# Head sums of the second half by accumulating DMAs instead of matmuls, with six weight loads held in pairs

## The chip, the cores and the metric

The kernel runs on one core of a Trainium2 chip. The metric is the device time of one execution in microseconds (us). Each kernel was also run once under the hardware profiler; numbers "from the profile" or "from the trace" belong to that one execution, and its span (first to last instruction) is about 2 us shorter than the time. Five engines work at once: TensorE (PE, matmuls), VectorE (DVE, elementwise), ScalarE (ACT, evictions and activations), GpSimd (POOL, here mostly an issuer of DMAs) and SyncE (SP, an issuer of DMAs).

## The reference

```python
x = A_x                                        # (1, 2048, 512), bf16
g = sigmoid((x * gate_w).sum(-1))              # one gate per position
# A: attention of 32 heads of 16; position s looks at s, s-2, ..., s-14 (8 offsets)
q, k, v = split(x @ wqkv)
logits  = einsum("bhsd,bhswd->bhsw", q, k[gathered]) * scale      # masked before 0
o       = einsum("bhsw,bhswd->bhsd", softmax(logits), v[gathered])
a       = o @ wo
# B: an MLP over the sequence axis
h = layernorm(x)                               # (2048, 512)
u = gelu(h^T @ w1 + b1)                        # w1: 2048 x 1792
b = (u @ w2 + b2)^T                            # w2: 1792 x 2048
return g * a + (1 - g) * b
```

The attention needs no large matmul besides the projections: each logit is a sum of 16 products. DVE does these products; PE does projections, both MLP matmuls and the output projection.

## The kernel before

The program records every operation with what it reads and writes. A list scheduler, which knows only estimated durations, then fixes the order on each engine, and semaphores are put in. So an engine works strictly through its list: an operation that must wait holds up all that stand behind it, on a DMA-issuing engine too.

The attention is worked in two halves of 1024 positions. For each half DVE forms products of q and shifted k in buffers `PB` of 128 x 8192 bf16, and adds the four slices of a head (`qk`, `qadd`). What is left is a sum over four neighbouring partitions, one per head. Before, PE does it for both halves, with a 0/1 matrix `RP` of 32 columns, and ACT copies the result out of PSUM:

```python
def f_sum(h, b0, with_gate):
    def fn(e):
        if with_gate:
            ...                                # 16 matmuls of the gate, first half only
        for wp in range(4):
            for c in range(4):                 # sum over 4 partitions: 128 rows -> 32 heads
                ins = e.matmul(ps[32*c:32*c+32, 4 + wp, :], lhsT=RP,
                               rhs=sub(PB[b0], ...), start=True, stop=True, tile_position=(0, 32*c))
        return ins
    return fn
...
A("pe",  f_sum(h, b0, h == 0), ...)
A("act", act(LOG[h], ps[:, 4:8, :], AF.Copy), 1.9, reads=LGB, writes=["log%d" % h], ...)
# then on DVE and ACT: max, subtract, exp, sum, normalise -> ATT[h]
for c in range(4):                             # "weight copies": one head's row to its 4 partitions
    prev = sch.dma("pool", ... e.dma_start(AVW[h] part c, ATT[h] rows 32c..32c+31, 4 times) ...)
```

Then come eight attention units of 256 positions. A unit is one product of 128 x 8192 (`m`), an addition of its halves (`a`, 128 x 4096), and two more (`b`, `c`). The result feeds the output projection of two output tiles: unit 4 feeds tiles 8 and 9. For three units the addition `a` is an accumulating DMA of 1 MB instead of a DVE instruction:

```python
AVD = (3, 4, 5)
def av_mult(u):
    AV(tt(pv, shifted V, AVW[...], ALU.mult), 4.4, ...)
    if u in AVD:
        sch.dma("pool", ... e.dma_start(pw(0, 4), pw(4, 4), accum_op=ALU.add) ...)
def av_add4(u):
    if u not in AVD:
        AV(tt(pw(0, 4), pw(0, 4), pw(4, 4), ALU.add), 2.25, ...)
```

W2 comes in eight loads of 0.92 MB on the queue of SP. Each waits only for its buffer to be free. The output tiles are stored from the same queue, through four store buffers: ACT cannot evict a tile before the store that used its buffer four tiles earlier has landed.

```python
def ld_w2(j):
    w1ld[7 + j] = load("w2_%d" % j, W2S[j], w2v[:, :, 256*j:256*j+256], ..., after=[w1ld[6 + j]])
def finish_tile(i):
    PE(f_wo(i, bank, 0, D), ..., ["ot%d" % (i // 2), "wo"], ...)         # output projection
    A("act", act(OUTS[:, i % 4, :], ps[:, bank, :], AF.Identity, ...))   # eviction
    sch.dma("sp", ... e.dma_start(outv[:, i, :], OUTS[:, i % 4, :]) ...) # store
```

Of the kernel before, what the change touches and what calls it, by code (L numbers as in the profile page):

```python
# [12 lines left out]
S = 2048  # L13
# [56 lines left out]
class _Sched:  # L70
# [73 lines left out]
    def _pass(self, ops, extra, dma_bw, dma_lat):  # L144
# [21 lines left out]
        dma_free = 0.0  # L166
# [8 lines left out]
        while nleft:  # L175
            best = None
            for e in self.ENGS:
                lst = ready[e]
                if not lst:
                    continue  # L180
                bo = None
                bk = None
                for op in lst:
                    st = max(clock[e], rtime[op.idx])
                    if op.table is not None and loaded is not None and op.table != loaded:
                        st += 1.3
                    k = (st, -bl[op.idx] + 3.0 * op.prio, op.idx)
                    if bk is None or k < bk:
                        bk = k
                        bo = op  # L190
                if best is None or bk < best[0]:
                    best = (bk, bo)
            assert best is not None, "scheduler deadlock (cyclic deps?)"
            st = best[0][0]
# [6 lines left out]
            if op.is_dma:  # L201
                clock[e] = st + op.dur
                xs = max(st + 0.3, dma_free)
                xd = max(op.nbytes / dma_bw, 0.05)
                dma_free = xs + xd
                op.end = max(dma_free, clock[e]) + dma_lat
            else:
                op.end = st + op.dur
                clock[e] = op.end
# [98 lines left out]
def bass_gated_mix__sliding_local_dilated__mixer_token_mlp__prompt_kernel(nc, A_x, A_wqkv, A_wo, B_x, B_w1, B_b1, B_w2, B_b2, gate_w, out, dbg=None):  # L308
    with contextlib.ExitStack() as es:
# [11 lines left out]
        for b in range(3):  # L321
# [42 lines left out]
        W1H = [view(n_, BF16, [(256, NST), (1, 256)], extra=k_ * W1N)  # L364
               for n_, k_ in (("W1", 0), ("W1", 1), ("W1", 2), ("XT", 0), ("XT", 1), ("W1", 0), ("W1", 1))]
        W1R = ["w1s0", "w1s1", "w1s2", "w1x0", "w1x1", "w1s0", "w1s1"]

        def w2view(name, extra=0):
            return view(name, BF16, [(256, NFT), (1, 256)], extra=extra)
# [166 lines left out]
        def ld_w1(j):  # L536
            w1ld[j] = load("w1_%d" % j, W1H[j], w1v[:, :, 256 * j:256 * j + 256], S * 256 * 2, [W1R[j]] + (XTALL if j in (3, 4) else []), order=j < 3,
                           after=[w1ld[j - 1]] if j > 3 else [])

        def ld_w2(j):  # L540
            w1ld[7 + j] = load("w2_%d" % j, W2S[j], w2v[:, :, 256 * j:256 * j + 256], F * 256 * 2, ["w2_%d" % j] + W2ALIAS[j], order=False,
# [40 lines left out]
        def f_q0(hb, dt):  # L582
            c0, c1 = ((0, 256), (256, 512), (0, 512))[hb]

            def fn(e):
                ins = None
                for dl in range(4):
# [26 lines left out]
        pe_q0(2, 3)  # L614
# [46 lines left out]
        kb0 = [bank_() for dl in range(2)]  # L661
        for k_ in range(2):
            for dl in range(2):
                PE(f_proj(1, dl, 0, kb0[dl], 2 * k_, 2 * k_ + 2), 0.44, XT0 + ["wk%d" % k_], ["b%d" % kb0[dl]], "pjk%d_0_%d" % (dl, k_))
                if k_ == 1:
                    evac(1, dl, 0, kb0[dl])
        for dl in range(2, 4):
            proj(1, dl, 0)
# [7 lines left out]
        for dl in range(4):  # L676
# [3 lines left out]
            if dl == 1:  # L680
                PE(f_tb, 0.06, ["b1r", "b2r", "gwr", "ident"], ["b3"], "t_b12")
                A("dve", lambda e: e.tensor_copy(out=GWREP, in_=sub(psb(3), 544, [(1, 4), (0, 32)])), 0.2, reads=["b3"], writes=["gwrep"], name="gwrep", prio=-20)
                A("dve", lambda e: e.tensor_copy(out=B1C, in_=psb(3)[:, 512:512 + NFT]), 0.15, reads=["b3"], writes=["b1c"], name="b1c", prio=-20)
                A("dve", lambda e: e.tensor_copy(out=B2C, in_=psb(3)[:, 528:528 + NST]), 0.15, reads=["b3"], writes=["b2c"], name="b2c", prio=-20)
# [20 lines left out]
        for t in range(NST):  # L705
            A("dve", (lambda t_: lambda e: e.tensor_scalar(out=X[:, t_, :], in0=X[:, t_, :], scalar1=col(RSTD, t_), scalar2=col(NMR, t_),  # L706
                                                           op0=ALU.mult, op1=ALU.add))(t), 0.33,
              reads=["rstd", "nmr", "st%d" % t], writes=["x%d" % t], name="ln%d" % t, prio=-10)


        def f_sum(h, b0, with_gate):
            def fn(e):
                ins = None
                if with_gate:
                    for dt in range(4):
                        for c in range(4):
                            ins = e.matmul(ps[32 * c:32 * c + 32, 3, :], lhsT=GWREP[:, dt, :],  # L717
                                           rhs=sub(XT, dt * S + c * UT_, [(HS, 2), (1, UT_)]),
                                           start=(dt == 0), stop=(dt == 3), tile_position=(0, 32 * c))
                for wp in range(4):  # L720
                    for c in range(4):
                        ins = e.matmul(ps[32 * c:32 * c + 32, 4 + wp, :], lhsT=RP, rhs=sub(PB[b0], (c // 2) * 4096 + 2 * wp * 512 + (c % 2) * UT_, [(512, 2), (1, UT_)]),  # L722
# [4 lines left out]
        LGB = ["b4", "b5", "b6", "b7"]  # L727
        PLAN = {0: (0, 1, 2), 1: (1, 2, 0)}
        PS = [["p%d_%d" % (b_, s_) for s_ in range(2)] for b_ in range(3)]
        qkd = {}  # L730
        for h in range(2):
            bb = PLAN[h]

            def qk(dl, b_, s_, h=h):
                sb = 2 * h + s_
                A("dve", tt(sub(PB[b_], s_ * 4096, [(512, NW), (1, 512)]), sub(QH[h], dl * HS + s_ * 512, [(0, NW), (1, 512)]),
                            sub(KH[h], dl * KR + PAD + s_ * 512, [(-2, NW), (1, 512)]), ALU.mult), 2.25,
                  reads=["q%d_%d" % (dl, sb), "k%d_%d" % (dl, sb)] + (["k%d_%d" % (dl, sb - 1)] if s_ else ["khalo" if h else "kpad"]),
                  writes=[PS[b_][s_]], name="qk%d_%d_%d" % (h, dl, s_))

            def qadd(x_, y_, s_, h=h):
                A("dve", tt(sub(PB[x_], s_ * 4096, [(1, 4096)]), sub(PB[x_], s_ * 4096, [(1, 4096)]), sub(PB[y_], s_ * 4096, [(1, 4096)]), ALU.add), 2.25,
                  reads=[PS[y_][s_]], writes=[PS[x_][s_]], name="qa%d_%d%d_%d" % (h, x_, y_, s_))
# [12 lines left out]
            for s_ in range(2):  # L756
                qk(3, bb[1], s_)
                qadd(bb[2], bb[1], s_)
            for s_ in range(2):
                qadd(bb[0], bb[2], s_)  # L760
            b0 = bb[0]
            A("pe", f_sum(h, b0, h == 0), 1.2 + (1.0 if h == 0 else 0), reads=PS[b0] + ["rp"] + ((XTALL + ["gwrep"]) if h == 0 else []),
              writes=LGB + (["b3"] if h == 0 else []), name="sum%d" % h, prio=-100, delay=0.2)
            if h == 0:
                A("act", act(E32, ps[:, 3, :], AF.Relu, scale=-1.0, bias=ZMAX), 0.6, reads=["b3"], writes=["e32"], name="zclip")
                A("act", act(EB, E32, AF.Exp, scale=-1.0, bias=ZMAX), 0.6, reads=["e32"], writes=["eb"], name="zexp", table=LOGEXP)
            A("act", act(LOG[h], ps[:, 4:8, :], AF.Copy), 1.9, reads=LGB, writes=["log%d" % h], name="lev%d" % h, prio=-30)
            if h == 0:
                A("dve", tt(psub(LOG[0], 0, 32, 0, [(UT_, NW), (1, PAD)]), psub(LOG[0], 0, 32, 0, [(UT_, NW), (1, PAD)]), MASK, ALU.add), 0.2,
                  reads=["mask"], writes=["log0"], name="msk", prio=-30)  # L770
            TR = ["s4", "s2", "s1"]
            A("dve", tt(M4, LOG[h][:, 0:4, :], LOG[h][:, 4:8, :], ALU.max), 0.65, reads=["log%d" % h], writes=["s4"], name="mx4_%d" % h, prio=-30)
            A("dve", tt(M2, M4[:, 0:2, :], M4[:, 2:4, :], ALU.max), 0.4, reads=["s4"], writes=["s2"], name="mx2_%d" % h, prio=-30)
            A("dve", tt(M1, M2[:, 0, :], M2[:, 1, :], ALU.max), 0.25, reads=["s2"], writes=["s1"], name="mx1_%d" % h, prio=-30)
            A("dve", tt(LOG[h], LOG[h], sub(M1, 0, [(0, NW), (1, UT_)]), ALU.subtract), 1.2, reads=["s1"], writes=["log%d" % h], name="msub%d" % h, prio=-30)
# [7 lines left out]
            A("dve", tt(ATT[h], ATT[h], sub(RB, 0, [(0, NW), (1, UT_)]), ALU.mult), 1.2, reads=["rb"], writes=["att%d" % h], name="nrm%d" % h, prio=-30)  # L783
# [3 lines left out]
            for c in range(4):  # L787
# [3 lines left out]
                               reads=["att%d" % h], writes=["avw%d_%d" % (h, c)] + al, after=[prev] if prev else [], name="av%d_%d" % (h, c))  # L791
                al = []
# [16 lines left out]
        AVD = (3, 4, 5)  # L809
        AVB = (2, 0, 1)  # L810
        avlast = [None]

        def AV(fn, dur, **kw):
            avlast[0] = A("dve", fn, dur, after=[avlast[0]] if avlast[0] else [], **kw)

        def av_parts(u):
            b_ = AVB[u % 3]
# [17 lines left out]
        def av_add(u):  # L835
            res, pv, pw = av_parts(u)
            AV(tt(pw(0, 2), pw(0, 2), pw(2, 2), ALU.add), 1.19, writes=res, name="avb%d" % u)
            AV(tt(OT[:, u], pv[:, 0], pv[:, 1], ALU.add), 0.66, reads=res, writes=["ot%d" % u, OTRES[u]], name="avc%d" % u)

        todo = []  # L840
        for u in range(8):
            av_mult(u)
            if todo and todo[0] + 2 <= u:
                av_add(todo.pop(0))
            if u in AVD:
                todo.append(u)
            else:
                av_add4(u)
                if todo and u == 7:
                    av_add(todo.pop(0))  # L850
                av_add(u)


        def f_ph2(ft, bank, half):
            def fn(e):
                ins = None
                for st in range(8 * half, 8 * half + 8):
                    ins = e.matmul(ps[:, bank, :], lhsT=W1H[ft // 2][:, st, 128 * (ft % 2):128 * (ft % 2) + 128], rhs=X[:, st, :],  # L858
                                   start=(st == 0), stop=(st == NST - 1))
# [3 lines left out]
        MLPB = [1, 2, 0, 1, 2, 0, 3, 1, 2, 0, 3, 1, 2, 0]  # L863
        for ft in range(NFT):
            bank = MLPB[ft]
            for half in range(2):
                PE(f_ph2(ft, bank, half), 1.735, ["x%d" % t for t in range(8 * half, 8 * half + 8)] + [W1R[ft // 2]], ["b%d" % bank],
                   "ph2_%d_%d" % (ft, half))
            A("act", act(UT[:, ft, :], ps[:, bank, :], AF.Gelu_apprx_tanh, bias=col(B1C, ft)), 0.7,
              reads=["b%d" % bank, "b1c"], writes=["ut%d" % ft] + (["wq0", "wq1", "wq2", "wq3", "wk0", "wk1", "wv"] if ft == 0 else []), name="gel%d" % ft, table=GELU)  # L870
            if ft % 2 == 1 and ft // 2 + 5 <= 6:
# [147 lines left out]
```

## Time and profile before

| before | value |
|---|---|
| time | 165.56 us, median of 3 (165.08 to 166.12) |
| span in the profile | 163.0 us |
| PE busy | 158.6 us, 97% |
| DVE busy | 151.1 us, 93% |
| last attention addition on DVE ends | 157.4 us |
| last matmul starts | 160.2 us |

This is the page of the kernel before. The second line gives each engine's busy time. The rows show 40 slices of the span: busy tenths of PE and DVE (9 is 90% or more) and the granted PE clock in tenths of full speed. The last line is the chain of work that ended last, by engine.

```profile
span 163.0 us, 1989 instructions
...
PE 158.6 (97%) x793; PEld 77.2 (47%) x808; DVE 151.1 (93%) x126; ACT 70.2 (43%) x100; POOL 12.0 (7%) x36
...
PE   7999999999999999999999999999999999999993
DVE  1789999999999999999999999999999999999961
...
PEclk9999999999999999999999999999999999999999
...
PE 97%; ACT 1%; issue 1%
...
```

PE and DVE are both full, but the chain that decides the end is 97% PE. The end of that chain of waits (start, duration, what ran):

```profile
...
152.13 3.06 PE ps L885 x28
155.19 4.33 PE ps L894 x20
159.54 1.34 ACT arena L453 x2
...
```

Lines L885 (second MLP matmul) and L894 (output projection) follow each other with no wait up to 159.5 us; only an eviction and a store come after. DVE, by contrast, is one unbroken group in its timeline from 83 to 157.4 us (start, duration, group; an idle would start a new line):

```profile
...
83.09 74.32 DVE L450 TENSOR_TENSOR arena<-arena 128x4096 bf16<-128x4096 bf16 x41
...
```

And the view of waits (who, for whom: us in total, times, longest) has next to nothing for PE and DVE between the start and the last tile; ACT waits much, but for PE, which costs nothing:

```profile
...
ACT arena L453 <- PE ps L894: 37.7, 11, 6.6
...
DVE arena L450 <- ACT arena L453: 0.6, 1, 0.6
...
PE ps L588 <- ACT arena L453: 0.2, 1, 0.2
...
```

So PE decides, and DVE has little slack.

### The profile page before, as it was taken

Reading aid. Unit: us, or ns where it says so; the run is one execution under the profiler, and the core shown is the slowest. Engines: PE = TensorE matmul, PEld = TensorE weight load, DVE = VectorE, ACT = ScalarE, POOL = GpSimd, SP = SyncE. Lnnn points to the kernel's source line nnn. Section 1 sums busy time; section 2 is a strip of 40 time slices with the busy share of each in tenths; the row PEclk is TensorE's granted clock in tenths of the full one; section 3 lists DMA queues with packets and bytes.
Section 4 is the critical chain, followed back from the end, with each engine's and each line's share of the span. In section 5 each row is a group of like instructions: output and inputs, shape, how many; then the busy total and the mean of one; then the engine's idle time right before and its main releaser. Section 6 shows DMA issues by size and latency. Waiting matters only on the chain.

```text
span 163.0 us, 1989 instructions
## 1 busy us (share of the span) xinstructions
PE 158.6 (97%) x793; PEld 77.2 (47%) x808; DVE 151.1 (93%) x126; ACT 70.2 (43%) x100; POOL 12.0 (7%) x36
## 2 busy tenths in 40 slices
PE   7999999999999999999999999999999999999993
PEld 4855555555544344444444344444444444444641
DVE  1789999999999999999999999999999999999961
ACT  3367677666771579662111348011111111111164
POOL 3000030020000000023000000003100222000000
PEclk9999999999999999999999999999999999999999
DMA  5999979729499095999998976981997899991014
GB/s 165 311 268 259 221 183 263 140 38 191 101 277 292 24 242 157 261 290 290 303 245 233 260 188 177 290 209 30 300 243 193 186 207 193 205 216 36 32 59 134
DMA packets 44685, 32.24 MB, mean 198 GB/s; under 512 B 7941, under 2 KB 42245, under 8 KB 44677
## 3 DMA queue, kind: packets, MB, share of 16 engines
q1 hardware_dynamic: 41444, 22.06, 51.6%
q0 software_dynamic: 2512, 9.44, 27.3%
q10 hardware_dynamic: 720, 0.62, 1.2%
q8 instruction: 6, 0.10, 0.2%
q14 instruction: 3, 0.02, 0.0%
HBM read 18.88 MB, written 2.10 MB: 129 GB/s over the span
## 4 chain that ended last, share of the span: by engine, by line
PE 97%; ACT 1%; issue 1%
PE ps L858 30%; PE ps L885 30%; PE ps L649 23%; PE ps L894 8%; PE ps L588 2%; PE ps L551 2%; PE ps L722 1%; ACT arena L453 1%; PE ps L717 1%; PE ps L567 1%; PE ps L604 0%
## 5 line engine op out<-in xcount | busy, mean ns | idle before, releaser
L450 DVE TENSOR_TENSOR arena<-arena 128x4096 bf16<-128x4096 bf16 (+8 forms) x79 | 131.9, 1718 | 1.6 <-ACT arena L453 0.6
L885 PE MATMUL ps<-arena 128*128 128x512 bf16 (+2 forms) x234 | 50.0, 366 | 0.2
L858 PE MATMUL ps<-arena 128*128 128x512 bf16 x218 | 48.5, 379 | 0.3
L453 ACT ACTIVATE arena<-ps,arena 128x512 bf16<-128x512 f32 (+1 forms) x30 | 21.8, 731 | 60.7 <-PE ps L894 37.7
L453 ACT ACTIVATE arena<-ps 128x512 bf16<-128x512 f32 (+3 forms) x53 | 32.9, 629 | 17.4 <-PE ps L649 10.9
L649 PE MATMUL ps<-arena 128*128 128x512 bf16 x173 | 38.0, 379 | 0.2
L885 PEld LDWEIGHTS ps<-arena 128*128 128x128 bf16 x238 | 22.8, 98 | 25.9
L858 PEld LDWEIGHTS ps<-arena 128*128 128x128 bf16 x224 | 21.7, 98 | 26.8 <-issue 0.8
L649 PEld LDWEIGHTS ps<-arena 128*128 128x128 bf16 x176 | 19.9, 113 | 18.0
L894 PE MATMUL ps<-arena 128*128 128x512 bf16 (+2 forms) x67 | 15.6, 366 | 0.1
L453 ACT ACTIVATE arena<-arena 128x16 f32<-128x16 f32 (+5 forms) x10 | 6.7, 678 | 9.7 <-DVE arena L450 9.6
L954 ACT ACT_TABLE_LOAD x7 | 9.0, 1283 | 2.8 <-issue 2.7
L894 PEld LDWEIGHTS ps<-arena 128*128 128x128 bf16 x68 | 6.5, 98 | 7.3
L692 DVE BATCH_NORM_STATS2 arena<-arena 128x6 f32<-128x512 bf16 x16 | 9.9, 679 | 0.1
L790 POOL DMA_DIRECT2D arena<-arena x8 | 4.3, 560 | 75.1 <-DVE arena L450 75.1
L706 DVE TENSOR_SCALAR arena<-arena 128x512 bf16<-128x512 bf16 x16 | 5.3, 404 | 0.0
L827 POOL DMA_DIRECT2D arena<-arena x3 | 3.6, 1209 | 17.7 <-DVE arena L450 17.7
L747 POOL DMA_DIRECT2D arena<-arena x2 | 2.5, 1268 | 30.6 <-DVE arena L692 20.2
L579 DVE CAST arena<-ps 128x256 bf16<-128x256 f32 x4 | 1.6, 422 | 3.2 <-PE ps L567 3.2
L588 PE MATMUL ps<-arena 128*128 128x256 bf16 (+1 forms) x27 | 3.8, 284 | 0.2 <-ACT arena L453 0.2
L551 PE MATMUL ps<-const-bfloat16-1.0 128*128 128x512 bf16 (+1 forms) x9 | 2.7, 483 | 0.8 <-PEq L1004 0.8
L588 PEld LDWEIGHTS ps<-arena 128*128 128x128 bf16 x28 | 2.9, 113 | 0.7 <-DVE arena L579 0.4
(30 smaller groups left out, 14.4 us busy)
## 6 DMA issues: line engine op xcount, KB each, us to landing
arena<-in_B_w_dram SPq DMA_DIRECT2D x7, 1024.0 KB, 6.8
arena<-in_B_w_dram SPq DMA_DIRECT2D x8, 896.0 KB, 9.4
arena<-arena POOLq DMA_DIRECT2D x5, 1024.0 KB, 9.7
arena<-arena POOLq DMA_DIRECT2D x8, 512.0 KB, 11.2
out_dram<-arena SPq DMA_DIRECT2D x15, 128.0 KB, 3.1
arena<-in_A_x_dram SPq DMA_DIRECT2D x3, 512.0 KB, 4.7
arena<-in_A_wqkv_dram SPq DMA_DIRECT2D x2, 256.0 KB, 3.8
arena<-in_A_wqkv_dram SPq DMA_DIRECT2D x1, 512.0 KB, 5.6
```

The lines of the kernel that those rows point to most:

```text
L450: return lambda e: e.tensor_tensor(out=o_, in0=a_, in1=b_, op=op_)
L453: return lambda e: e.activation(out=o_, in_=i_, func=f_, **kw)
L551: ins = e.matmul(ps[:, 7, 0:n_], lhsT=C1, rhs=nc.const_aps.tensor(1.0, (128, n_), BF16), start=True, stop=True)
L588: ins = e.matmul(ps[:, dl, c0:c1], lhsT=sub(WQKV, dt * 3 * D + dl, [(4, 128)]), rhs=XT[:, dt, c0:c1], start=(dt == 0 and hb == 0), stop=(d ...
L649: ins = e.matmul(ps[:, bank, :], lhsT=sub(WQKV, dt * 3 * D + tn * D + dl, [(4, 128)]), rhs=XT[:, dt, sb * 512:(sb + 1) * 512], start=(dt = ...
L692: A("dve", (lambda t_: lambda e: e.bn_stats(out=ST6[:, t_, :], in_=X[:, t_, :]))(t), 0.67, reads=["x%d" % t], writes=["st%d" % t], name="s ...
L706: A("dve", (lambda t_: lambda e: e.tensor_scalar(out=X[:, t_, :], in0=X[:, t_, :], scalar1=col(RSTD, t_), scalar2=col(NMR, t_), op0=ALU.mu ...
L790: prev = sch.dma("pool", (lambda d_, s_: lambda e: e.dma_start(d_, s_))(dst, src), 524288, sch.dsem("av%d_%d" % (h, c)), issue=1.0, reads= ...
L858: ins = e.matmul(ps[:, bank, :], lhsT=W1H[ft // 2][:, st, 128 * (ft % 2):128 * (ft % 2) + 128], rhs=X[:, st, :], start=(st == 0), stop=(st ...
L885: ins = e.matmul(ps[:, bank, 0:c1 - c0], lhsT=W2S[i // 2][:, ft, 128 * (i % 2):128 * (i % 2) + 128], rhs=UT[:, ft, c0:c1], start=(ft == 0) ...
L894: ins = e.matmul(ps[:, bank, 0:c1 - c0], lhsT=OT[:, i // 2, dl, 128 * (i % 2):128 * (i % 2) + 128], rhs=WO[:, dl, c0:c1], start=False, sto ...
L954: e.preload_act_table_set(want)
```

## The change

Its intent is to take the second half's head sums (16 matmuls) and their eviction off PE, PSUM and ACT. Each sum over four partitions becomes a fold: four accumulating DMAs of 256 KB (`fa`: partition p+2 onto p), four plain copies of 128 KB into the logits (`fb`), then four accumulating DMAs of 128 KB (`fc`: partition p+1). These landings come in series, so queues should be free meanwhile: W2 loads 2 to 7 are held in pairs, the first pair until the last `fa` has landed, the second until the last `fc`, the third until the second of the second half's weight copies. Units 2, 4, 5 (instead of 3, 4, 5) now add by DMA, and the units' instructions have a new order, with unit 0 and two products left as filler while the folds run. Besides, W1 (but for its first load) and W2 are loaded in rows of 1 KB instead of 512 bytes, the PSUM bank plan, the scheduler's estimates for DMAs and the order of the last tiles are new, the gate's matmuls go ahead of the sums, and eight layer-norm writes go from DVE to ACT. Cut to its core:

```diff
 def ld_w2(j):
-    ... w2v[:, :, 256*j:256*j+256] ...
+    ... w2v[:, 7*(j%2):7*(j%2)+7, 512*(j//2):512*(j//2)+512] ...
+        deps={2: folds[0:1], 4: folds[1:2], 6: [avw[1, 1]]}.get(j, []),
@@ layer norm writes
+    if t >= NST - 8:
+        A("act", act(X[:, t, :], X[:, t, :], AF.Identity, scale=..., bias=...), ...)
@@ sums
-    A("pe", f_sum(h, b0, h == 0), ...)                  # both halves
-    A("act", act(LOG[h], ps[:, 4:8, :], AF.Copy), ...)
+    if h:
+        for s_ in range(2):
+            for k_ in range(2):
+                fas[s_] = fold("fa...", PB rows k_, k_+4, ..., += PB rows k_+2, ..., accumulate)
+        for s_ in range(2):
+            for k_ in range(2):
+                for c in (2*s_, 2*s_+1):
+                    fl = fold("fb" if k_ == 0 else "fc", LOG rows 32c.., PB rows k_.., accumulate if k_ == 1)
+        folds += [fas[1], fl]
+    else:
+        A("pe", f_sum(b0), ...); A("act", ... AF.Copy ...)
@@ attention units
-AVD = (3, 4, 5)
+AVD = (2, 4, 5)
+AVHOLD = {"ava1": msb[1], "avm3": nrm[1]}
+AVORDER = "m0 a0 b0 c0 m1 m2 a1 b1 c1 m3 a3 b3 c3 b2 c2 m4 m5 m6 b4 c4 a6 b6 c6 m7 b5 c5 a7 b7 c7"
@@ last output tiles ("m": second MLP matmuls of tile, half; "w": output projection of tile)
+TAILORDER = [("m",12,0), ("m",13,0), ("w",8), ("m",14,0), ("m",15,0,0), ("w",9), ("m",15,0,1), ("m",12,1), ...]
```

`AVHOLD` keeps unit 1's additions behind the subtraction of the second softmax.

## The prediction

> **What bounds it now.** TensorE. The busy table gives PE 158.6 us of a 163.0 us span (97%); the chain of waits is 97% PE, back to back; the waits view charges PE 1.0 us in all, none after 5 us. In the chain, 128x512 matmuls follow each other every 0.2156 us until 159.5 us; then come evictions and the store. The clock is full in every slice. DVE is close behind (151.1 us, 93%, no idle worth naming): its last attention add ends at 157.4 us in the timeline, and the output projection that reads it starts near 158.6: 1.2 us of slack.
>
> **What the change does.**
> 1. PE: the second half's head sums go (16 matmuls of 32 columns, 0.98 us in the chain). The gate's 16 move forward, nothing saved. All other matmuls keep number and shape, in another order. Expected: -0.98 us, all critical.
> 2. DVE: eight layer-norm writes go to ACT (0.32 us each in sequence, -2.6 us); the first product starts about 0.4 us sooner. Long adds and products are the same in number. ACT (43% busy) loses a 1.88 us eviction and absorbs this.
> 3. DMA: four accumulating folds of 256 KB, four copies and four accumulates of 128 KB replace sum and eviction: three landings in series. The 1 MB accumulates here took 7.8 to 13.1 us to land. The Trainium skill (DMA: Bandwidth & Descriptors, Anatomy of one DMA) gives 2.0 us fixed plus size; here undisturbed 128 KB stores took 1.67 us. Estimate, from these and 0.55 to 1.2 us of POOL issue each: 12 to 16 us from the last add to the last fold.
> 4. W1/W2 rows become 1 KB instead of 512 B; W2 loads 2 to 7 are held so that folds and weight copies find free queues.
>
> **Critical path after.** I add trace durations in the new DVE order: last second-half add near 87 us, then unit 0 and products 1 and 2 (17 us of filler) until 104. The folds should end at 99 to 103, just hidden. Then softmax, renormalisation near 115, weight copies (first 7.8 us in before; needed 10 us later), last attention add near 154.5. PE, one us shorter, needs it at 156.8. W2 pairs: needed near 109, 124.6 and 140, released near 92, 101 and 125; loads took 5.3 to 16 us. So I expect no new PE wait, and the gain is just the removed sums. The DVE gain becomes slack.
>
> **Predicted: 164.6 us** (165.56 - 0.98), 80% range 163.8 to 166.2. Faster by over 2%: 0.02. Within 2%: 0.92. Slower by over 2%: 0.06.
>
> **What would show each step.**
> - PE busy near 157.6 us, no wait over 0.3 us after the start; one block of 16 sum matmuls, not two; span near 162.0.
> - DVE's last add at 153.5 to 156 us; its wait on the last fold 0 to 2 us near 104; folds landing in 3 to 6 us each.
> - W2 pairs landing well before use; PE pace still 0.216 us.
> - No PE wait on ACT during projections.
>
> **What would make it wrong.** Folds much slower than 16 us (32 strided partitions, queued behind a weight copy): DVE stands, all behind it shifts as much, and beyond about 2 us PE waits in the tail. A held W2 pair landing late stops PE outright. A late accumulate for units 4 or 5 (8.7 us allowed, 7.8 to 13.1 seen) stops DVE for some us. A gain over 2% would need PE to lose 3.3 us; there is no such work to lose.

## The result, and the profile after

The time after is 171.87 us (median of 4, 171.39 to 172.57), with 165.39 us for the kernel before in the same rounds (165.08 to 166.12). The ratio is 1.0389, 95% interval 1.0337 to 1.0440: slower. Here and below a ratio is the mean time of one kernel's runs over that of the other's runs of the same rounds, so it is not quite the ratio of the medians quoted. Executions over 1.5% slower than the fastest of the same kernel are left out of the means. The predicted range ended at 166.2 us.

The page after, in the same lines as before:

```profile
span 170.0 us, 1969 instructions
...
PE 160.2 (94%) x777; PEld 77.1 (45%) x792; DVE 149.0 (88%) x118; ACT 69.7 (41%) x105; POOL 21.5 (13%) x48
...
PE   7999999999999999999999999999999999099993
DVE  1699799999999999999999998398999998499940
...
PEclk9999999999999999999999999999999999759999
...
DVE 42%; DMA 31%; PE 10%; SPq 7%; issue 6%; POOL 1%; ACT 1%; DVEq 0%; POOLq 0%
...
```

PE's row has a digit 0 that was not there: a slice of 4.25 us in which PE did nearly nothing. In that slice and the next the clock row falls to 7 and 5. And the chain is no longer PE's: DVE and DMA hold 73% of it. The chain itself, cut to its DMA steps and its end (start, duration, what ran):

```profile
...
72.13 15.01 DMA arena<-arena
87.43 6.25 DMA arena<-arena
...
96.49 7.96 DMA arena<-arena
104.74 4.29 DMA arena<-arena
...
135.47 11.26 DMA arena<-arena
...
149.17 1.49 PE ps L935 x3
150.65 4.26 PE ps L926 x14
...
166.59 1.34 ACT arena L455 x2
...
```

The first four DMA steps are the folds: an `fa` landing at 87.1 us, 15 us after it was issued, two copies `fb`, and an `fc` that lands at 109.0 us. The step at 135.47 us is the accumulating DMA of unit 4, 11.26 us long. From there the line is straight: DVE adds, and at 149.17 us PE starts the output projection L935. The 14 matmuls of L926 that follow take 4.26 us.

The waits that are new, from the view of waits:

```profile
...
ACT arena L455 <- DMA out_dram<-arena: 12.6, 3, 8.3
...
DVE arena L452 <- DMA arena<-arena: 6.6, 2, 3.6
...
PE ps L935 <- DVE arena L452: 4.9, 1, 4.9
...
```

DVE's timeline shows where its two waits for DMA lie; the bracket is the idle time ahead of the group and what ended it:

```profile
...
109.16 9.46 DVE L452 TENSOR_TENSOR arena<-arena 128x1024 bf16<-128x1024 bf16 x11 [3.64 <-DMA arena<-arena]
119.10 24.74 DVE L452 TENSOR_TENSOR arena<-arena 128x2048 bf16<-128x2048 bf16 x10 [0.48 <-ACT arena L455]
146.76 16.52 DVE L452 TENSOR_TENSOR arena<-arena 128x2048 bf16<-128x2048 bf16 x11 [2.92 <-DMA arena<-arena]
```

3.64 us for the last fold and 2.92 us for unit 4's accumulate. PE shows a single real stop:

```profile
...
143.01 1.24 PE L926 MATMUL ps<-arena 128*128 128x512 bf16 x5
149.17 1.49 PE L935 MATMUL ps<-arena 128*128 128x512 bf16 x3 [4.91 <-DVE arena L452]
150.45 4.47 PE L926 MATMUL ps<-arena 128*128 128x512 bf16 x14
...
```

14 matmuls of L926 span 4.47 us here; in a run below with hardly a stop (e2) the same 14 take 2.81 us. In the trace, ten matmuls in a row start 0.427 us apart after the stop, where 0.2156 us is normal. One record is missing just here: the tile has four matmuls of L935, and three are recorded. Its first weights were loaded at 148.76 us, so the stop was nearer 4.5 than 4.91 us, and eleven matmuls ran at the slow pace. The numbers below are those of the records. The Trainium skill ("TensorE: Matmul & The Clock Gate", What's actually happening) says that an idle array falls back to half its clock after an idle window of about 3.4 us. The same page (Wait — 56ns, not 53.3ns?) gives 426.7 and 215.7 ns start to start for 512 columns. This trace agrees, with 0.427 and 0.2156 us, the slow pace after 4.91 us of recorded idle.

The loss can be placed by PE's stages, with starts read from the traces:

| PE (us) | before | after | difference |
|---|---|---|---|
| first projection matmul | 8.59 | 8.99 | +0.40 |
| from there to the first matmul of the second MLP matmul | 89.42 | 88.92 | -0.50 |
| from there to the start of the last matmul | 62.15 | 69.29 | +7.14 |

In the middle row the removed sums are seen: -0.98 us, of which new waits, mostly in front of the moved gate (two matmuls 0.65 us apart), take back about half. The last row is the loss: two matmuls start 5.29 us apart where 0.22 us is due, which is +5.07 us, and ten at half clock are 10 x 0.211 = +2.1 us. (With the missing record counted it is about 4.7 and 2.3 us.)

SP's timeline shows the held third pair. L496 are the loads, L948 the stores of output tiles:

```profile
...
119.76 2.38 SPq L948 DMA_DIRECT2D out_dram<-arena  x2
130.19 0.39 SPq L496 DMA_DIRECT2D arena<-in_B_w_dram  x1
130.62 2.29 SPq L948 DMA_DIRECT2D out_dram<-arena  x1
132.95 0.84 SPq L496 DMA_DIRECT2D arena<-in_B_w_dram  x1
133.83 6.44 SPq L948 DMA_DIRECT2D out_dram<-arena  x4
```

The second weight copy lands at 130.17 us, and at 130.19 and 132.95 us the two loads go out, 0.92 MB each. The stores behind them in the list could not be issued before 130.6 us. In the trace's DMA records (issue to landing) the two loads take 8.5 and 12.3 us, unit 4's accumulate, issued at 135.5 us, takes 11.3, and the stores issued between 133.8 and 140 us take 13 to 15 us. Before, loads 6 and 7 had landed by 121 us.

Two theories are open. One: the third hold brought two loads into the stretch of unit 4's accumulate and the stores, and that is nearly all of the loss; the folds do only a little. The rival: the folds are the loss, because they came 6 to 10 us late and delayed all of DVE behind them. Further rivals came up on the way.

### The profile page after: what moved, and what is told of

Its sections match the earlier page's. It is cut to its first block, busy times and chain, and to the rows that moved or that the text cites. A ratio compares the mean times of both kernels' runs of the same rounds, so it can differ in the third digit from the quotient of the medians.

```text
span 170.0 us, 1969 instructions
## 1 busy us (share of the span) xinstructions
PE 160.2 (94%) x777; PEld 77.1 (45%) x792; DVE 149.0 (88%) x118; ACT 69.7 (41%) x105; POOL 21.5 (13%) x48
## 4 chain that ended last, share of the span: by engine, by line
DVE 42%; DMA 31%; PE 10%; SPq 7%; issue 6%; POOL 1%; ACT 1%; DVEq 0%; POOLq 0%
DVE arena L452 39%; DMA arena<-arena 26%; PE ps L926 6%; SPq L495 6%; DMA arena<-in_A_x_dram 4%; PE ps L935 4%; DVE arena L708 2%; DVE arena L690 1%; SPq L496 1%; POOL arena L787 1%; ACT arena L455 1%; DVE arena L680 0%; DVE arena L701 0%; DVE arena L697 0%; DVE arena L682 0%
## 5 line engine op out<-in xcount | busy, mean ns | idle before, releaser
L452 DVE TENSOR_TENSOR arena<-arena 128x4096 bf16<-128x4096 bf16 (+7 forms) x79 | 132.6, 1719 | 8.5 <-DMA arena<-arena 6.6
L926 PE MATMUL ps<-arena 128*128 128x512 bf16 (+2 forms) x236 | 51.7, 375 | 0.1
L926 PEld LDWEIGHTS ps<-arena 128*128 128x128 bf16 x238 | 23.3, 100 | 27.6 <-issue 2.6
L455 ACT ACTIVATE arena<-ps 128x512 bf16<-128x512 f32 (+3 forms) x52 | 30.4, 604 | 12.1 <-PE ps L653 6.6
L894 PEld LDWEIGHTS ps<-arena 128*128 128x128 bf16 x224 | 21.9, 98 | 26.6 <-issue 0.4
L653 PEld LDWEIGHTS ps<-arena 128*128 128x128 bf16 x176 | 19.7, 113 | 18.3 <-ACT arena L455 0.4
L455 ACT ACTIVATE arena<-arena 128x512 bf16<-128x512 bf16 (+6 forms) x18 | 13.3, 739 | 22.5 <-DVE arena L452 21.6
L935 PE MATMUL ps<-arena 128*128 128x512 bf16 (+2 forms) x64 | 15.8, 378 | 5.1 <-DVE arena L452 4.9
L787 POOL DMA_DIRECT2D arena<-arena x12 | 9.6, 859 | 24.2 <-DMA arena<-arena 23.6
L935 PEld LDWEIGHTS ps<-arena 128*128 128x128 bf16 x68 | 6.6, 100 | 12.3 <-DVE arena L452 5.0
L828 POOL DMA_DIRECT2D arena<-arena x8 | 4.7, 605 | 50.5 <-DVE arena L452 50.5
L759 POOL DMA_DIRECT2D arena<-arena x2 | 2.5, 1267 | 28.3 <-DVE arena L690 21.3
L867 POOL DMA_DIRECT2D arena<-arena x3 | 3.7, 1226 | 16.0 <-DVE arena L452 15.8
(31 smaller groups left out, 17.4 us busy)
## 6 DMA issues: line engine op xcount, KB each, us to landing
arena<-arena POOLq DMA_DIRECT2D x4, 256.0 KB, 11.1
```

Of the source, the lines that this page charges most:

```text
L452: return lambda e: e.tensor_tensor(out=o_, in0=a_, in1=b_, op=op_)
L455: return lambda e: e.activation(out=o_, in_=i_, func=f_, **kw)
L653: ins = e.matmul(ps[:, bank, :], lhsT=sub(WQKV, dt * 3 * D + tn * D + dl, [(4, 128)]), rhs=XT[:, dt, sb * 512:(sb + 1) * 512], start=(dt = ...
L787: return sch.dma("pool", lambda e: e.dma_start(o_, i_, **kw), nb, sch.dsem(name), issue=1.1, reads=reads, writes=writes, name=name, after= ...
L828: prev = sch.dma("pool", (lambda d_, s_: lambda e: e.dma_start(d_, s_))(dst, src), 524288, sch.dsem("av%d_%d" % (h, c)), issue=1.0, reads= ...
L894: ins = e.matmul(ps[:, bank, :], lhsT=w_, rhs=X[:, st, :], start=(st == 0), stop=(st == NST - 1))
```

## The experiments

Eleven kernels ran, on several chips, always beside the kernel before, all correct but one. The ratio is to the kernel before of the same call, so ratios may be compared across chips.

| run | what | time, us | ratio to before [95%] |
|---|---|---|---|
| changed kernel | | 171.87 | 1.0389 [1.0337, 1.0440] |
| e2_pair3_free | third hold off | 166.95 | 1.0091 [1.0028, 1.0153] |
| e4_no_holds | all holds off | 174.39 | 1.0527 [1.0474, 1.0580] |
| e1_pair1_later | first pair held until the last fold | 175.13 | 1.0550 [1.0483, 1.0617] |
| e3_sums_on_pe | sums back on PE | 188.06 | 1.1340 [1.1291, 1.1390] |
| e5_sums_placed | sums back on PE, placed well; no holds | 165.83 | 1.0022 [1.0004, 1.0040] |
| e6_pair1_on_copy | third off, first until the copies | 167.62 | 1.0143 [1.0107, 1.0178] |
| e7_before_hold3 | kernel before plus the third hold | 175.32 | 1.0603 [1.0561, 1.0645] |
| e8_tail_late | tiles 8 and 9 projected later | 176.09 | 1.0643 [1.0595, 1.0691] |
| e9_small_pair3 | third hold kept, its loads 1/7 | 168.07 | 1.0082 [1.0057, 1.0106] |
| e10_unit1_filler | third off, more filler for the folds | 165.59 | 1.0026 [0.9984, 1.0069] |
| e11_tile8_later | the same, tile 8 later | 166.41 | 1.0028 [0.9990, 1.0066] |

### Which hold

All four kernels are the changed kernel with one edit in the line of holds, or in the line of sums.

```diff
 deps of W2 loads:
-    {2: folds[0:1], 4: folds[1:2], 6: [avw[1, 1]]}
+    {2: folds[0:1], 4: folds[1:2]}              # e2_pair3_free
+    {2: folds[1:2], 4: folds[1:2], 6: [avw[1, 1]]}   # e1_pair1_later
+    []                                          # e4_no_holds
```

> The changed kernel, with the third pair of W2 loads (6, 7) not held on the second weight copy (load 7 still waits for its place in SBUF, near 119 us). Theory A (that pair, released at 130.2 us, shares the DMA engines with the accumulate of unit 4): the accumulate lands in 9.5 us or less (11.3 in the changed kernel), VectorE's idle before unit 4's next add falls from 2.9 us to 1.2 us or less, TensorE's wait for that add from 4.9 us to about 3, time 169 to 170.7 us. Rival C (8.6 us between product and next add is too little for this accumulate anyway): idle 2.5 us or more, time within 0.7 us of 171.9.

Measured: 166.95 us (166.28 to 168.5). Unit 4's accumulate takes 8.1 us instead of 11.3, DVE has no wait for it, and the clock stays full. PE's stop of 4.91 us is now 0.47 us, less than expected:

```profile
...
141.58 3.19 PE L926 MATMUL ps<-arena 128*128 128x512 bf16 x14
145.23 1.04 PE L935 MATMUL ps<-arena 128*128 128x512 bf16 x4 [0.47 <-DVE arena L452]
146.10 2.81 PE L926 MATMUL ps<-arena 128*128 128x512 bf16 x14
...
```

DVE still stands 3.34 us for the folds, which land at 108.5 us as in the changed kernel. So one dependency of eight loads is worth 4.9 us of the 6.5 us lost, with the folds as late as before. The rival that the late folds alone are the loss falls.

> The changed kernel, with none of the six W2 loads held: each goes when its place in SBUF is free. Theory A (W2 traffic lengthens the folds; the hold on the first pair ends too early): the loads now run beside the first folds as well, the last fold lands at 108 us or later, while the accumulate of unit 4 lands in 9.5 us or less; time 169 to 172 us. Rival E (the holds themselves did the harm): last fold at 105 us or earlier and time under 168 us.

Measured: 174.39 us (173.54 to 175.24), above the expected range. Last fold at 112.4 us; DVE stands 6.8 us ahead of the softmax; PE stands 5.0 us near 150 us, so here too the clock falls. The idea that holding loads does harm as such falls: the first two holds are worth 7.4 us (174.39 against 166.95 us on the same chip), and the third costs 4.9 us.

> The changed kernel, with the first held W2 pair (loads 2, 3) released by the last fold's landing, as the second pair is, instead of by the last of the four first-stage folds. Theory A (that pair, released at 96.4 us in the changed kernel, shares the DMA engines with the last three folds, whose landings took 8.0, 6.6 and 4.3 us): the last fold lands at 104.5 us or earlier (109.0 before), the idle of VectorE before the softmax of the second half falls from 3.6 us to 1 us or less, and the time falls to 167 to 169.5 us; TensorE may now wait 0 to 2 us for load 2 near 110 us. Rival B (the folds queue behind one another and behind the weight copies on their own queue; W2 traffic does not matter): last fold still at 107.5 us or later, idle at least 2.5 us, time 171 us or more.

Measured: 175.13 us (174.08 to 176.42). The fold part came near what was expected: with no held load in flight until 105.2 us the folds end at 106.0 us and DVE stands 0.9 us. That is 15.4 us after the third `fa` was issued at 90.6 us, but 18.1 us after the last addition (87.9 us): two copies stand ahead of that `fa` in POOL's list, and they waited for the first `fa`, which landed at 89.2 us. The time was missed by far. Four loads were now released together at 105 us, and loads 3, 4 and 5 took 13, 15 and 27 us; PE stood 2.4 us for weights, and 5.0 us for ACT, which waited 13.5 us for a store. What was taken from the folds was given back to loads and stores. This is the first sign of a second way from slow DMAs to PE: store, store buffer, eviction, PSUM bank, PE.

> The changed kernel, with the second half's head sums back on TensorE and its eviction back on ScalarE; no folds, so the first two pairs of W2 loads have nothing to be held on; the third stays held; all the rest of the change kept. Theory A (the fold chain is the main cause): VectorE does not wait before the softmax, TensorE's wait in the tail falls from 4.9 us to 1.5 us or less, the clock stays full, time 165 to 167 us. Rival D (the new W1/W2 layout, the third hold and the new order of the tail are the cause): TensorE still waits 3 us or more in the tail, time 170 us or more.

```diff
-            if h:          # folds
+            if False:      # sums of both halves by matmul
```

Measured: 188.06 us, and not an answer to its question. The changed bank plan puts tiles of the first MLP matmul in the four PSUM banks that the sums need, so the scheduler put the second sums ahead of those tiles and PE stood 17.2 us for DVE. It shows only that the removal of the sums also freed four banks that the new plan relies on.

### Sums back, in a good place

> The changed kernel, with the second half's head sums back on TensorE, this time put by hand behind the last group's first half (near 90 us, when VectorE has the products ready; in e3 the same sums stood in front of matmuls that share their PSUM banks, and TensorE waited 17 us), its eviction back on ScalarE, and no W2 load held. Layout, bank plan, order of the tail and units 2, 4, 5 stay as in the changed kernel. Theory A (the folds and the traffic released by the holds are the whole loss): VectorE idles under 1 us before the second softmax, TensorE waits under 1 us in all after its start, time 164.8 to 166.5 us, that is as before. Rival D (the new layout, bank plan or order of the tail costs too): 168 us or more.

```diff
-            if h:
+            if False:
@@ place: after the first half of the last tile of the first MLP matmul, once its banks are read
+            if (ft, half) == (13, 0):
+                sums[1].order.add(chain[0]); sums[1].deps.update(gels.values()); chain[0] = sums[1]
@@ W2 loads
-    deps={2: folds[0:1], 4: folds[1:2], 6: [avw[1, 1]]}
+    deps=[]
```

Measured: 165.83 us (165.59 to 166.23), ratio 1.0022. PE has no wait after its start, DVE no wait over 1 us for DMA. So the wider rows, the bank plan, the new order of tiles and units and the layer norm on ACT, taken together, cost at most 0.4% net: the rival that they were the loss falls. The loss lies in what the folds brought with them.

### The third hold alone, and where it reaches PE

> The kernel before, with only one thing added: loads 6 and 7 of W2 wait for the second weight copy of the second half, as in the changed kernel; no folds. Theory A (the release puts 1.8 MB of loads beside the accumulates): both loads go near 122 us, the accumulates of units 3 and 4 (7.8 and 10.0 us before) land in 10 us or more each, VectorE, which had no idle there, idles 2 to 5 us behind them, TensorE waits 1 us or more in the tail, time 166.8 to 169.5 us. Rival F (the third hold harms only together with the folds): within 0.7 us of the time before.

```diff
 # in the kernel before
+    deps=[avw11[0]] if j == 6 else [],    # avw11: the second half's second weight copy
```

Measured (e7): 175.32 us (174.45 to 176.84), ratio 1.0603. The mechanism is as expected and the size was missed: it costs 9.8 us, with no fold in the program. Loads 6 and 7 go out at 121.8 and 122.8 us and take 11 and 28 us; the three accumulates take 12.0, 13.2 and 14.5 us; a store takes 23.5 us. Here the stop comes by the second way:

```profile
...
ACT arena L453 <- DMA out_dram<-arena: 17.4, 1, 17.4
...
PE ps L888 <- ACT arena L453: 6.5, 1, 6.5
...
DVE arena L450 <- DMA arena<-arena: 3.7, 1, 3.7
...
```

ACT waits 17.4 us for a store, and PE 6.5 us for the bank that ACT should have emptied. The rival that the hold harms only in company with the folds falls. In this trace SP also took from 127.80 to 138.77 us to issue that store, behind load 7, and issued nothing else meanwhile; so in this kernel bytes and order are not told apart.

> The changed kernel, with the output projections of tiles 8 and 9 moved back behind the last matmuls of the MLP, so that TensorE asks for units 4 and 5 some 5 us later. Theory A (VectorE's lateness is the cause, the early place of tile 8 only where it shows): VectorE's idle before the softmax and behind the accumulate of unit 4 stays (3.6 and 2.9 us), its last add stays within 1 us of 163.3 us, TensorE still waits 2 us or more in the tail, time 169 to 171.7 us. Rival G (the early place of tile 8 in the tail is the cause): under 168 us.

```diff
-TAILORDER = [m12.0, m13.0, w8, m14.0, m15.0a, w9, m15.0b, m12.1, m13.1, m14.1, ...]
+TAILORDER = [m12.0, m13.0, m14.0, m15.0a, m12.1, m13.1, m14.1, w8, m15.0b, ...] + [w9, w10, ...]
```

Measured (e8): 176.09 us (174.95 to 177.36), a miss: it was to be no slower than the changed kernel. DVE's two idles stay (4.8 and 2.9 us). PE no longer stands for DVE at tile 8, but it stands longer, for ACT:

```profile
...
ACT arena L455 <- DMA out_dram<-arena: 15.0, 2, 12.3
...
PE ps L926 <- ACT arena L455: 9.0, 2, 8.1
...
```

So the early place of tile 8 in the list is not what made the loss. In the changed kernel the stop at tile 8 hides a second one of the same cause behind it: stores that land near 153 us.

> e2 (third pair not held), and the first pair released by the last plain copy of the fold chain, between the two earlier choices. Theory A: the last fold lands at 105 to 107.5 us (108.5 in e2), VectorE's idle before the softmax falls from 3.3 us to 2 us or less, its last attention add ends at 157 to 158.7 us instead of 159.7, TensorE waits under 0.5 us for load 2, and the time is 165.2 to 166.4 us (166.95 in e2), so at most as fast as before. Rival B (the folds are slow on their own): last fold at 108 us or later, time 166.5 us or more.

```diff
-    {2: folds[0:1], 4: folds[1:2], 6: [avw[1, 1]]}
+    {2: folds[2:3], 4: folds[1:2]}         # folds[2]: the last plain copy fb; third hold off
```

Measured over five rounds (e6): 167.62 us (167.24 to 169.39), a miss. The first pair goes out at 100.15 us, and now meets the last two `fc` accumulates, which take 7.6 and 7.9 us (3.4 to 3.7 us without loads beside them in e1). The last fold lands at 109.1 us, as in the changed kernel. The release point moved the collision but did not take it away.

### Bytes, or order in the queue?

The held loads can do harm in two ways: their bytes share the DMA engines, or they stand in front of the stores in SP's list. One kernel keeps the order and cuts the bytes:

> The changed kernel with the third hold kept exactly where it is, but the two held loads carry one of their seven chunks (128 KB each instead of 0.92 MB); the result is wrong on purpose. It separates two ways in which the held loads do harm. Theory T (traffic: the loads' bytes share the DMA engines with the accumulate of unit 4 and with the stores): the accumulate of unit 4 lands in at most 9 us instead of 11.3, the stores behind the loads in at most 10 us instead of 14 to 15, DVE's 2.9 us idle near 146.8 is under 1 us, PE waits under 1.5 us, no half clock, 166.3 to 168.5 us, close to the run without the third hold (166.95). Rival Q (order: the stores stand behind the held loads in the sync engine's queue until 130 us, whatever the loads carry): the third store is still issued near 130, evictions still wait over 8 us for stores, PE waits over 3 us, 170 us or more. The store's issue time itself should stay near 130 us in both; what tells them apart is whether that late issue alone stops PE.

```diff
-    load("w2_%d" % j, W2S[j],                             w2v[:, 7*(j%2):7*(j%2)+7, ...], ...)
+    load("w2_%d" % j, W2S[j][:, 0:1, :] if j > 5 else W2S[j], w2v[:, 7*(j%2):7*(j%2)+(1 if j > 5 else 7), ...], ...)
```

This is e9. The result is wrong: most of the last weights are never loaded. SP's list and its times are those of the changed kernel:

```profile
...
130.96 0.34 SPq L496 DMA_DIRECT2D arena<-in_B_w_dram  x1
131.35 2.62 SPq L948 DMA_DIRECT2D out_dram<-arena  x1
134.01 0.97 SPq L496 DMA_DIRECT2D arena<-in_B_w_dram  x1
...
```

The time is 168.07 us (median of 4); two of the four runs, the profiled one among them, count as slow, and the two fast ones are 166.39 and 167.11 us. Unit 4's accumulate takes 8.2 us, DVE has no wait for it, and the stores issued at 131 to 136 us land in 2.6 to 6.0 us, though issued no earlier than in the changed kernel, but for half a microsecond. The two fast runs lie beside e2 (ratios 1.0082 and 1.0091). So in the changed kernel the bytes lengthen the accumulate and the stores; the order alone does not. The Trainium skill ("DMA: Bandwidth & Descriptors", Issuing engines are not separate DMA queues) says that DMAs issued by SP, ACT and POOL all run on the same 16 DMA engines and interleave; this pair of runs agrees: with 1.6 MB less on SP's queue, an accumulate issued by POOL goes from 11.3 to 8.2 us. One expectation was missed: PE still stood 2.36 us in the profiled run, and half clock followed. The fold chain ended at 109.8 us there, DVE stood 4.62 us for it, and PE waited for DVE at tile 8:

```profile
...
109.92 9.46 DVE L452 TENSOR_TENSOR arena<-arena 128x1024 bf16<-128x1024 bf16 x11 [4.62 <-DMA arena<-arena]
...
146.52 1.04 PE L935 MATMUL ps<-arena 128*128 128x512 bf16 x4 [2.36 <-DVE arena L452]
...
```

So in this run late folds stopped PE with no wait for unit 4.

### What is left: the folds

> Third hold removed (as in the run without it), and DVE's 2.3 us long add of unit 1 moved in front of the second softmax, where DVE stood 3.3 us for the last fold; nothing else moves. If the fold chain's extra length is what is left of the loss, DVE's idle before the softmax falls from 3.3 to about 1 us, the last attention add moves from 159.7 to 157 to 158.3 us, PE waits under 0.3 us after its start, and the time is 165.0 to 166.5 us: at most level with the kernel before, with the removed sums' 0.98 us showing as a span near 162.5 to 163.5. If instead the time stays at 166.7 or more with the idle gone, the rest of the loss is not the folds' but of PE's order or the late start.

```diff
 # third hold off, as in e2_pair3_free
-AVHOLD = {"ava1": msb[1], ...}
+# after scheduling: move ava1 (unit 1's long addition) ahead of the second softmax's first maximum
```

Measured over five rounds (e10): 165.59 us (165.09 to 167.52), ratio 1.0026 with 1 inside its interval. DVE's wait for the last fold falls from 3.34 to 1.94 us and the wait for unit 4 is 0.23 us (DVE's timeline):

```profile
...
109.16 3.87 DVE L458 TENSOR_TENSOR arena<-arena 128x1024 bf16<-128x1024 bf16 x5 [1.94 <-DMA arena<-arena]
...
117.70 24.74 DVE L458 TENSOR_TENSOR arena<-arena 128x2048 bf16<-128x2048 bf16 x10 [0.48 <-ACT arena L461]
142.67 16.53 DVE L458 TENSOR_TENSOR arena<-arena 128x2048 bf16<-128x2048 bf16 x11 [0.23 <-DMA arena<-arena]
...
```

PE's stages: 9.44 us to the first projection matmul, 88.58 us to the second MLP matmul, 62.93 us to the last. The removed sums do show, as -0.84 us in the middle stage (89.42 before). But 0.48 us at tile 8 and 0.29 us at a later tile, where PE waits for DVE, give them back (start to start, less the usual 0.2156 us; as idle they are 0.31 and 0.12 us), and this execution started 0.85 us later.

> The best version so far (third hold removed, unit 1's long add in front of the softmax) with tile 8's output projection one block of seven matmuls (1.5 us) later; nothing else moves on any engine. In the version without this shift PE still stood 0.48 us for that tile and 0.29 us for a later one. If those waits are the rest of what hides the removed sums' 0.98 us, the first wait is gone, the span is 162.5 to 163.5 us and the time 164.6 to 165.5 us, at or just below the kernel before. If the time does not move (165.4 to 166.2), the rest is the later start of the projections and the last attention add, which this shift does not touch.

```diff
-TAILORDER = [m12.0, m13.0, w8, m14.0, ...]
+TAILORDER = [m12.0, m13.0, m14.0, w8, ...]
```

Measured over five rounds (e11): 166.41 us (164.8 to 167.98; ratio 1.0028). The wait at tile 8 is gone, but in the profiled run unit 4's accumulate took 11.1 us without the third hold, DVE stood 2.71 us for it, and PE stood 0.9 and 0.7 us near the end (start to start, as above). One of its six runs counts as slow. W2 load 7, issued at 117.6 us, landed only at 137.1 us in the profiled run.

```profile
...
143.75 16.52 DVE L458 TENSOR_TENSOR arena<-arena 128x2048 bf16<-128x2048 bf16 x11 [2.71 <-DMA arena<-arena]
...
```

Two things follow. The third hold is not the only way to an accumulate of 11 us. And nearly the same wait of DVE (2.92 us in the changed kernel) cost much less here: DVE had no wait for the folds before it and reached unit 4's next addition at 143.8 us instead of 146.8, and PE asked for tile 8 1.5 us later. In the changed kernel the two waits, 3.64 and 2.92 us, add up in front of tile 8. So this variant has no use: what is left swings with how the DMAs happen to meet, and no kernel here beats the kernel before.

## Why the prediction was wrong, point by point

- **"PE: the second half's head sums go ... Expected: -0.98 us, all critical."** Right as a count. The sums are gone, and with the third hold off and more filler 0.84 us are seen in that stage. It was the only gain, as predicted.
- **"DVE: eight layer-norm writes go to ACT", "No PE wait on ACT during projections".** Right. With sums back and holds off (e5) the rest of the change is within 0.4% of before.
- **"Estimate ...: 12 to 16 us from the last add to the last fold."** Too short. The addition ended at 88.2 us (87 was predicted), the last fold landed at 109.0: 20.8 us. With no held load beside them they still took 18.1 us (e1): 2.7 us while POOL's list was held up in front of the third `fa`, and then 15.4, which lie inside the estimate. The held loads added to this. In the changed kernel the first pair of loads, released at 96.4 us by the last `fa`, ran beside the last two copies and the last two accumulates; from the issue of the third `fa` to the last landing it is 20.5 us here and 15.4 in e1. DVE stood 3.6 us for the folds. Their share of the time is about 1 us: 166.95 against 165.59 us when filler was added (different chips, and the intervals of the two ratios overlap, so this share is only likely). It swings: in e6's profiled run (169.39 us, counted as fast) a fold wait of 4.4 us with only 0.96 us for unit 4 stopped PE for 3.1 us, and in e9's (169.02 us, counted as slow) one of 4.6 us alone stopped it for 2.4 us.
- **The failed step: "W2 pairs: needed near 109, 124.6 and 140, released near 92, 101 and 125 ... So I expect no new PE wait".** The loads did come in time: PE never waited for a weight. But that was the wrong test. The third pair, released at 130.2 us rather than 125, put 1.84 MB on the DMA engines while unit 4's accumulate and five stores were in flight. The accumulate took 11.3 us where 8.7 were allowed, DVE stood 2.9 us on top of its 3.6 us for the folds, and PE stood 4.91 us by the records, then ran at half clock for ten matmuls: 7.1 us. Taking that hold away gives back 3.0% of the time, or 4.9 us (e2); putting it alone in the kernel before costs 9.8 us (e7); keeping it with a seventh of the bytes takes DVE's wait for unit 4 away (e9).
- **"last attention add near 154.5. PE ... needs it at 156.8."** The last addition ended at 163.3 us, and the slack was read at the wrong place. The first tile that could stop PE was tile 8, whose projection the new order puts at 144 us. Even without the third hold it had no slack: PE stood 0.47 us there (e2).
- **What would make it wrong.** The list named the mechanism ("a late accumulate for units 4 or 5 ... stops DVE for some us") but took 7.8 to 13.1 us from the kernel before as the range for it, without asking what the change itself puts beside it; and it stopped at DVE. That PE then loses its clock, and that stores and evictions form a second way to PE, was not in it.

What stays open: the start of the projections lay at 8.6 us in the one profile of the kernel before, and at 8.9 to 9.8 us in all others, e7 (before plus one hold) with 9.0 among them. This looks like the landing of the first loads, which varies from run to run, but no run settles it. In the changed kernel itself the share of the folds and of the third hold can't be added up exactly, since both delay the same chain. No run has the third hold and quick folds in the changed kernel with all else in place: e1 comes nearest, but there four loads were released at once.

## What to carry to other kernels

A held load must be checked against what it will meet, not only against who needs it: list every DMA that will be in flight when it is released, and what stands behind those. Read the slack at each hand-over between engines, not at the last one, and count stops of PE such as those of 2.4 to 8.1 us here with the half clock that followed them. When an experiment takes pressure off one queue point and the time does not fall, look for where the same bytes now collide.

## What the Trainium skill lacked or had wrong

- "DMA: Bandwidth & Descriptors", Anatomy of one DMA: its fit for a DMA issued by GpSimd is 2.0 us plus bytes/436e3 us. An estimate from it for 1 MB is 4.4 us; the accumulates of 1 MB here took 7.8 to 13.1 us before and 7.9 to 12.7 after. For 128 KB it gives an estimate of 2.3 us; the last two accumulates of e1, with hardly a load beside them, took 3.4 and 3.7 us. It says that DMAs interleave but has no figure for how much longer one takes beside others: 128 KB stores took 1.67 us at the end of the kernel, and 13 to 15 us beside the held loads.
- The same page has none for DMAs issued by POOL one behind the other: the first two `fa` folds, issued at 72 to 73 us among the weight copies and with W2 loads in flight, landed 15.0 and 17.8 us later, the next two, issued at 88.5 and 89.1 us with the copies nearly done, in 7.2 us.
- "TensorE: Matmul & The Clock Gate", What's actually happening: the idle window of about 3.4 us is not needed in full as one stop. In e9 PE stood 2.36 us, ran at nearly full pace again for 1.1 us, and only then did six matmuls start 0.427 us apart; in e6 it stood 3.08 us by the records (2.8 us by its weight loads, as one matmul record is missing), and seven followed; in the changed kernel it was 4.91 us and ten. After 1.65 us (e1) and 0.47 us (e2) there were none. The two paces are as the page says.
- No page that we found follows a slow store to PE through store buffers, evictions and PSUM banks; here this stopped PE for 5.0 to 8.1 us in three kernels (e1, e7, e8).
